# Early attention output turned by PE transposes and summed out of one bf16 bank, q and k turned by DMA and scored in one block from pair 8 on

## The chip, the cores and the metric

One core of a Trainium2 chip runs the whole program. The metric is device time in microseconds of one execution, given as the median of several runs. The engines named below are PE (matrix multiply; PEld is its weight load), DVE (vector), ACT (scalar), POOL (GpSimd) and SP (which only issues transfers here). They run side by side, each in the order of its own queue, and wait for one another on semaphores.

## The reference

Attention over 8 batches, 8 heads, 576 tokens and 64 dimensions, made of two parts, then a two-layer block without bias:

```
local:  softmax(q k^T / 8) v  over keys with |i - j| < 4
down:   q, k and v averaged over groups of 4 tokens; softmax(qd kd^T / 8) vd
x = local + repeat(down, 4)        # heads side by side: 4608 tokens x 512
h = x @ w_in                       # 512 -> 2048
out = (h - tanh(h)) @ w_out        # 2048 -> 512, f32
```

## The kernel before, in words

Work comes in 32 pairs of heads; pair p is batch p // 4, heads 2(p % 4) and the next. One pair (`attention(p)`) goes through these steps.

1. Load and cast. SP loads q and k (`qkn`) and v in overlapping windows (`vst`); `prep_v` casts v to bf16 (`vw`). `qkn` is cast to bf16 in `qr`: on any of three engines for pairs 0 to 3, on POOL at L515 after that.
2. Turn. q and k are needed with the dimension on the partitions. Pairs below `T_DMA` = 12 do that with nine PE transposes (L547) and two copies out of PSUM (L551). Later pairs do it with a DMA transpose (L531, `qT<-qr`) and one copy on ACT (L534).
3. Pool. Two adds (L564, L569, mostly POOL) make the averaged q and k, `qkd`.
4. Score. `s1` is eight matmuls of 120 query columns (L584) into two PSUM banks (token `t1`); `s2` is two more of 96 columns and four of 144 columns on `qkd` (L606) into two others (`t2`). Pairs from `NEW` = 12 on issue both as one block, `s12`.
5. Exp and mask. Pairs 0 to 3 add a bias to the scores on PE (L589). From pair 4 on, ACT takes the exponential out of PSUM into `E` (L622, L634, L637), and DVE then multiplies `E`, in SBUF, by a 0/1 `mask` (L626 with 960 columns, L641 with 192).
6. Output. 18 matmuls of 65 columns (L650, L657) give both outputs and the sums in two banks. DVE takes reciprocals (L670) and scales into `ln` (L672): five tiles of local output and two of the averaged one.
7. Turn back. Pairs below `X_DMA` = 12: nine matmuls (`back`, L683, L685, L692) multiply `ln` by an identity, and the averaged tiles by a matrix `up` that repeats each row four times, so that PSUM sums both in f32 in two banks; one copy (L720 on DVE or L721 on ACT) makes `xT`. Later pairs: a DMA transpose (L696, `lT<-ln`) and two adds (L703, L709) on DVE or POOL.

The dense block takes `xT` in nine blocks of 512 tokens: `mm1` (L734) 64 matmuls of 512 columns, then ACT's tanh (L742) and DVE's subtraction into `gT` (L745); `mm2` (L760) 64 matmuls, ACT's copy to `y` (L771) and a store (L774).

No order is written by hand. `Program` holds every step with an engine, an estimated duration and its dependencies. `order` plays the program with these estimates, with a latency for each engine (`LAT`), and with a cap on the PSUM banks that each kind of step may hold (`P.cap`: 6 of the 8 for pairs from 4 on, 4 for the dense block). `choice` lets it pick the engine. What comes out is a fixed queue for each engine. An engine whose next instruction isn't ready waits, even if later ones are.

Of the kernel before, what the change touches and what calls it, by code (L numbers as in the profile page):

```python
# [23 lines left out]
class Program:  # L24

    LAT = {"PE": 270, "ACT": 150, "DVE": 110, "POOL": 150, "SP": 50, "DMA": 2200}
    RING = 230

    def __init__(self):
        self.ops = []  # L30
        self.alternatives = {}
        self.slack = []
        self.soon = set()
        self.goal = set()
        self.ring = {}
        self.rings = {}
        self.touch = []
        self.use = []
        self.toks = []
        self.cap = {}  # L40
        self.last_write = {}
        self.readers = {}
# [66 lines left out]
    def order(self):  # L109
# [56 lines left out]
        for i in range(n):  # L166
            if left[i] == 0:
                make_ready(i)
        for step in range(n):
            best = None  # L170
            for eng, cand in ready.items():
                if not cand:
                    continue
                now = max(free.get(eng, 0.0), min(at[i] for i in cand))
                if eng == "PE":
# [8 lines left out]
                else:  # L184
                    pick = min((self.ops[i][4], i) for i in cand if at[i] <= now)[1]
# [12 lines left out]
            end = now + self.ops[i][1]  # L198
            want = [t for t in self.use[i] if t.first == i]
# [57 lines left out]
def kernel(  # L257
# [9 lines left out]
    nc = tc.nc  # L267
# [31 lines left out]
    mask = fixed("mask", [128, 576], BF16)  # L299
# [19 lines left out]
    up = lT[1].rearrange("p n c -> p (n c)")[:, 0:S]  # L319
    r = fixed("r", [128, 2, 7], FP32, 2)  # L320
    ln = fixed("ln", [128, 7, 128], BF16, 2)
# [31 lines left out]
    def c_up():  # L353

        GP.memset(up, 1.0)
        GP.affine_select(out=up, in_=up, compare_op=ALU.is_ge, fill=0.0,
                         base=0, pattern=[[1, S]], channel_multiplier=-4)
        GP.affine_select(out=up, in_=up, compare_op=ALU.is_ge, fill=0.0,
                         base=3, pattern=[[-1, S]], channel_multiplier=4)

# [8 lines left out]
    def c_mask():  # L369

        GP.memset(mask, 1.0)
        m4 = mask[:, 0:480].rearrange("p (t c) -> p t c", c=QW)
        for part, pat in ((m4, [[0, 4], [1, QW]]),
                          (mask[:, 480:576], [[1, 96]])):
            neg = [[-s, n] for s, n in pat]
            GP.affine_select(
                out=part, in_=part, compare_op=ALU.is_ge, fill=0.0,
                base=-1, pattern=neg, channel_multiplier=1)
            GP.affine_select(
                out=part, in_=part, compare_op=ALU.is_ge, fill=0.0,  # L380
                base=7, pattern=pat, channel_multiplier=-1)
        GP.affine_select(
            out=mask[:, 0:QW], in_=mask[:, 0:QW], compare_op=ALU.is_ge,
            fill=0.0, base=-4, pattern=[[0, QW]], channel_multiplier=1)
        GP.affine_select(
            out=mask[:, 480:576], in_=mask[:, 480:576], compare_op=ALU.is_ge,
            fill=0.0, base=99, pattern=[[0, 96]], channel_multiplier=-1)
# [80 lines left out]
    def pool_v4(p):  # L468
# [9 lines left out]
        op("POOL", 1150, a1, reads=[("v4", s)], writes=["v2"], pri=10 * p - 12)  # L478
        op("POOL", 750, a2, reads=["v2"], writes=[("vp", s)], pri=10 * p - 12)

    def pool_v(hb):
# [15 lines left out]
        op("ACT", 590, lambda: A.copy(  # L497
# [5 lines left out]
    def attention(p):  # L503
# [10 lines left out]
        if p >= NEARLY:  # L514
            op("POOL", 1300, lambda: GP.tensor_copy(  # L515
# [14 lines left out]
        if p >= T_DMA:  # L530
            P.dma("SP", 1740, lambda: nc.sync.dma_start_transpose(  # L531
                out=qT[s], in_=qr[s].rearrange("p a c -> p (a c)")), 1300, 72,
                  src=[("qr", s, 0), ("qr", s, 1)], dst=[("qT", s)], pri=-50, lead=500)
            op("ACT", 1250, lambda: A.copy(  # L534
# [3 lines left out]
        else:  # L538
            for a0, a1, tn, cn in ((0, 5, 290, 740), (5, 9, 230, 620)):
# [10 lines left out]
                def copy(fn, a0=a0, a1=a1, b16=b16):  # L550
# [5 lines left out]
                          ("DVE", cn, lambda copy=copy: copy(V.tensor_copy))][:1 + (p < NP)],  # L556
# [10 lines left out]
        def add2(eng):  # L567
            with nc.allow_low_precision("pooled q and k"):
                eng.tensor_tensor(out=qkd[s][:, 0:G],  # L569
                                  in0=half[:, :, 0, :],  # L570
                                  in1=half[:, :, 1, :], op=ALU.add)
        P.choice([(name, n1, lambda eng=eng: add1(eng)) for name, n1, _, eng in adders],
# [41 lines left out]
        if new:  # L614
            op("PE", 620, s12, slack=late, reads=qks + [("qkd", s)], fill=[t1, t2], pri=pri)
        else:
            op("PE", 420 * cold + 250 * (p < NP), s1, slack=late,
# [4 lines left out]
        op("ACT", 960, lambda: A.activation(  # L622
            out=e1, in_=two(t1)[:, :, 0:480], func=AF.Exp, scale=SCALE),
           drain=[t1], writes=[("E", e, 0)], pri=pri)
        if p >= NP:
            op("DVE", 950, lambda: V.tensor_tensor(  # L626
                out=e1, in0=e1,
                in1=mask[:, 0:480].unsqueeze(1).to_broadcast([128, 2, 480]),
                op=ALU.mult), reads=["mask"], writes=[("E", e, 0)], pri=pri)
        yield  # L630
        if not new:
            op("PE", 380 * cold + 100 * (p < NP), s2, slack=late, reads=qks + [("qkd", s)],
               fill=[t2], pri=pri)
        op("ACT", 310, lambda: A.activation(  # L634
            out=e2v, in_=two(t2)[:, :, 0:96], func=AF.Exp, scale=SCALE),
           drain=[t2], writes=[("E", e, 1)], pri=pri)
        op("ACT", 650, lambda: A.activation(  # L637
            out=e3, in_=two(t2)[:, :, 96:384], func=AF.Exp, scale=SCALE / 16.0),
           drain=[t2], writes=[("E", e, 2)], pri=pri)
        if p >= NP:  # L640
            op("DVE", 450, lambda: V.tensor_tensor(  # L641
                out=e2v, in0=e2v,
                in1=mask[:, 480:576].unsqueeze(1).to_broadcast([128, 2, 96]),
                op=ALU.mult), reads=["mask"], writes=[("E", e, 1)], pri=pri)
# [25 lines left out]
        op("DVE", 200, lambda: V.reciprocal(out=r[s], in_=blocks()[:, :, :, 64]),  # L670
           drain=[to], writes=[("r", s)], pri=pri)
        op("DVE", 1060, lambda: V.tensor_tensor(  # L672
# [6 lines left out]
        tb = P.psum(2, kind)  # L679

        def back():
            for half in range(2):
                T.matmul(two(tb)[:, half, 0:288], ln[s][:, 5, :], up[:, 288 * half:288 * half + 288],  # L683
                         start=True, stop=False)
            T.matmul(two(tb)[:, 1, 224:288], ln[s][0:16, 6, :], up[0:16, 0:64],  # L685
                     start=False, stop=False)
            for t in range(NT):
                q0, q1 = QW * t, QW * t + NQ[t]
                for half in range(2):
                    c0, c1 = max(q0, 288 * half), min(q1, 288 * half + 288)  # L690
                    if c0 < c1:
                        T.matmul(two(tb)[:, half, c0 - 288 * half:c1 - 288 * half],  # L692
                                 ln[s][0:NQ[t], t, :], ident[0:NQ[t], c0 - q0:c1 - q0],
                                 start=False, stop=(t == (2, NT - 1)[half]))
        if p >= X_DMA:
            P.dma("SP", 1350, lambda: nc.sync.dma_start_transpose(  # L696
# [4 lines left out]
            def join(eng):  # L701
# [12 lines left out]
            P.choice([("DVE", 1900, lambda: join(V)), ("POOL", 1400, lambda: join(GP))],  # L714
                     reads=[("lT", s)], writes=[("x", b, j)], pri=pri)
            return
        op("PE", 450 * cold, back, slack=late, reads=[("ln", s), ("lT", 1), "ident"],
           fill=[tb], pri=pri)
        xs = xT[j][:, b * S:(b + 1) * S].rearrange("p (n c) -> p n c", n=2)
        P.choice([("DVE", 720, lambda: V.tensor_copy(out=xs, in_=two(tb)[:, :, 0:288])),  # L720
                  ("ACT", 680, lambda: A.copy(out=xs, in_=two(tb)[:, :, 0:288]))],  # L721
                 drain=[tb], writes=[("x", b, j)], pri=pri)
# [4 lines left out]
    def mm1(kb, fc):  # L727
# [14 lines left out]
        op("ACT", 590, lambda: A.activation(  # L742
            out=u[us], in_=one(tok), func=AF.Tanh),
           drain=[tok], writes=[("u", us)], pri=DPRI)
        op("DVE", 670, lambda: V.tensor_tensor(  # L745
# [6 lines left out]
    def mm2(kb, i):  # L752
        ts, part, g = i // 4, i % 4, kb % 2
        if part == 0:
# [190 lines left out]
```

The softmax here doesn't subtract the row's maximum and nothing guards it: scores larger than these inputs give would overflow.

## Time and profile before

| What | Value |
|---|---|
| median of 7 runs | 333.99 us (332.46 to 339.42) |
| the profiled execution's own time | 336.19 us |
| its span in the trace | 334.2 us |
| PE busy | 315.2 us (94%) |
| DVE busy | 212.6 us (64%) |
| ACT busy | 202.9 us (61%) |
| POOL busy | 177.2 us (53%) |
| data moved | 59.80 MB, most of it before 225 us |
| first dense matmul | 25.52 us |
| last dense matmul ends | 329.81 us |

The span runs from the first instruction to the last. The first 25 us prepare batch 0. After that PE always has dense work behind it, with the attention of later batches between; from 250 us on it has dense work alone. Busy time of an engine includes time in which it is held inside an instruction, so a mean duration above the usual one is worth a look.

### The profile page before, as it was taken

To read this page: it belongs to the slowest core of one execution; us is meant where nothing else is said; L and a number is where in the kernel's file an instruction comes from. 1 tells how busy PE (TensorE), PEld (TensorE's weight loads), DVE (VectorE), ACT (ScalarE), POOL (GpSimd) and SP (SyncE) were. 2 spreads that over 40 slices of the span, in tenths; PEclk is the share of its full clock that TensorE was granted. 3 is DMA by queue.
4 is the path that set the end of the run, shared out by engine and by line. 5 is a ranking of instruction groups with operands and counts; after the bars stand their busy time and mean duration, and the time that the engine had idled before them with its cause. 6 is when DMAs were issued, how large, how long until landed. Compare 5 with 4: busy or idle time off the path is not lost.

```text
span 334.2 us, 6505 instructions
## 1 busy us (share of the span) xinstructions
PE 315.2 (94%) x2420; PEld 158.8 (48%) x2461; DVE 212.6 (64%) x330; ACT 202.9 (61%) x334; POOL 177.2 (53%) x211
## 2 busy tenths in 40 slices
PE   7989999999999999999696999999999999999994
PEld 2554555564444544444353445444444444444441
DVE  4868765479966969678969877758763344433300
ACT  3968864588777866687665466877544443444411
POOL 8564548859667698869887849887310000000000
PEclk9999999999999999999999999999999999999999
DMA  7999999989999999999999999982320001000021
GB/s 237 272 220 217 237 258 257 291 263 249 280 218 269 219 201 241 223 233 234 244 227 227 278 218 266 207 216 61 90 59 33 31 31 63 33 31 31 33 94 64
DMA packets 108862, 59.80 MB, mean 179 GB/s; under 512 B 86174, under 2 KB 96030, under 8 KB 108830
## 3 DMA queue, kind: packets, MB, share of 16 engines
q1 hardware_dynamic: 104318, 54.60, 69.8%
q0 software_dynamic: 4224, 4.19, 7.7%
q10 hardware_dynamic: 288, 0.59, 0.5%
q8 instruction: 19, 0.31, 0.4%
q14 instruction: 13, 0.11, 0.1%
HBM read 43.64 MB, written 9.44 MB: 159 GB/s over the span
## 4 chain that ended last, share of the span: by engine, by line
PE 72%; DVE 13%; DMA 6%; ACT 4%; POOL 2%; issue 2%; POOLq 0%; DVEq 0%; ACTq 0%
PE bank L734 31%; PE bank L760 29%; DMA lT<-ln 3%; DVE ln L672 3%; DVE E L626 3%; DMA w_out_sb<-in_moe_w_out_dram 3%; DVE E L641 3%; PE bank L650 3%; PE bank L584 2%; DVE gT L745 2%; PE bank L657 2%; ACT E L622 2%; DVE xT L703 1%; PE bank L692 1%; PE bank L683 1%
## 5 line engine op out<-in xcount | busy, mean ns | idle before, releaser
L734 PE MATMUL bank<-xT,w_in_sb 128*128 128x512 bf16 x557 | 143.7, 379 | 1.4 <-DVE gT L745 0.3
L760 PE MATMUL bank<-w_out_sb,gT 128*128 128x512 bf16 x555 | 141.6, 379 | 2.1 <-issue 0.6
L745 DVE TENSOR_TENSOR gT<-bank,u 128x512 bf16<-128x512 f32 x144 | 97.2, 685 | 64.1 <-ACT u L742 63.6
L742 ACT ACTIVATE u<-bank 128x512 f32<-128x512 f32 x144 | 85.9, 598 | 76.7 <-PE bank L734 73.8
L760 PEld LDWEIGHTS <-gT 128*128 128x128 bf16 x576 | 53.9, 98 | 62.8 <-issue 0.7
L734 PEld LDWEIGHTS <-w_in_sb 128*128 128x128 bf16 x576 | 53.9, 98 | 61.9 <-issue 0.5
L564 POOL TENSOR_TENSOR half<-qk 128x576 f32<-128x576 bf16 x28 | 32.1, 1145 | 21.0 <-ACT qk L551 12.3
L626 DVE TENSOR_TENSOR E<-E,mask 128x960 bf16<-128x960 bf16 x28 | 32.8, 1171 | 11.3 <-ACT E L622 11.1
L622 ACT ACTIVATE E<-bank 128x960 bf16<-128x960 f32 x32 | 31.1, 972 | 12.9 <-PE bank L584 12.8
L515 POOL CAST qr<-qkn 128x1152 bf16<-128x1152 f32 x28 | 32.2, 1151 | 9.9 <-DMA qT<-qr 6.7
L672 DVE TENSOR_TENSOR ln<-bank,r 128x896 bf16<-128x896 f32 x32 | 34.7, 1087 | 0.9
L771 ACT COPY y<-bank 128x512 f32<-128x512 f32 x36 | 21.1, 586 | 19.5 <-PE bank L760 19.0
L451 POOL CAST vw<-vst 128x640 bf16<-128x640 f32 x31 | 25.7, 833 | 8.5 <-DMA vst<-in_v_dram 8.5
L472 POOL TENSOR_TENSOR v<-v 72x512 f32<-72x512 f32 x20 | 25.4, 1270 | 2.8 <-DMA v<-in_v_dram 2.0
L534 ACT COPY qk<-qT 128x1152 bf16<-128x1152 bf16 x20 | 24.1, 1203 | 4.2 <-DMA qT<-qr 4.2
L650 PE MATMUL bank<-vw,E 128*128 128x65 bf16 x320 | 20.1, 194 | 4.8 <-DVE E L641 2.2
L569 POOL TENSOR_TENSOR qkd<-half 128x288 bf16<-128x288 f32 x29 | 21.8, 752 | 1.3 <-DVE r L670 0.4
L650 PEld LDWEIGHTS <-E 128*128 128x128 bf16 x320 | 16.6, 98 | 11.9 <-DVE E L641 2.9
L476 POOL TENSOR_TENSOR vp<-v 72x256 bf16<-72x256 f32 x20 | 14.5, 727 | 13.8 <-PE bank L657 13.6
L637 ACT ACTIVATE E<-bank 128x576 bf16<-128x576 f32 x32 | 21.1, 659 | 0.0
L703 POOL TENSOR_TENSOR xT<-lT 128x480 bf16<-128x480 bf16 x11 | 11.2, 1016 | 13.9 <-DMA lT<-ln 13.8
L641 DVE TENSOR_TENSOR E<-E,mask 128x192 bf16<-128x192 bf16 x28 | 18.0, 642 | 0.7 <-ACT E L634 0.7
(75 smaller groups left out, 220.8 us busy)
## 6 DMA issues: line engine op xcount, KB each, us to landing
vst<-in_v_dram SPq DMA_DIRECT2D x62, 160.0 KB, 5.2
qkn<-in_q_dram SPq DMA_DIRECT2D x32, 288.0 KB, 5.4
out_dram<-y SPq DMA_DIRECT2D x36, 256.0 KB, 4.6
qkn<-in_k_dram SPq DMA_DIRECT2D x30, 288.0 KB, 5.8
v<-in_v_dram SPq DMA_DIRECT2D x20, 288.0 KB
w_in_sb<-in_moe_w_in_dram POOLq DMA_DIRECT2D x4, 512.0 KB, 12.4
w_out_sb<-in_moe_w_out_dram POOLq DMA_DIRECT2D x4, 512.0 KB, 10.1
qkn<-in_k_dram ACTq DMA_DIRECT2D x2, 288.0 KB, 3.1
```

The lines of the kernel that those rows point to most:

```text
L451: P.choice([(eng, ns, lambda fn=fn: fn(out=vw[w][:, 2 * jj:2 * jj + 2, :, 0:64], in_=vst[s])) for eng, ns, fn in CAST_V[p >= NEARLY]], rea ...
L515: op("POOL", 1300, lambda: GP.tensor_copy(out=qr[s].rearrange("p a (h d) -> p h a d", h=2), in_=qkn[sn].rearrange("p h (a d) -> p h a d", ...
L564: eng.tensor_tensor(out=half, in0=four[:, :, 0:2, :], in1=four[:, :, 2:4, :], op=ALU.add)
L622: op("ACT", 960, lambda: A.activation(out=e1, in_=two(t1)[:, :, 0:480], func=AF.Exp, scale=SCALE), drain=[t1], writes=[("E", e, 0)], pri=pri)
L626: op("DVE", 950, lambda: V.tensor_tensor(out=e1, in0=e1, in1=mask[:, 0:480].unsqueeze(1).to_broadcast([128, 2, 480]), op=ALU.mult), reads= ...
L641: op("DVE", 450, lambda: V.tensor_tensor(out=e2v, in0=e2v, in1=mask[:, 480:576].unsqueeze(1).to_broadcast([128, 2, 96]), op=ALU.mult), rea ...
L650: T.matmul(two(to)[:, hh, 65 * t:65 * t + 65], E[e][:, c:c + 128], vw[w][:, 2 * jj + hh, t, :], start=True, stop=True)
L672: op("DVE", 1060, lambda: V.tensor_tensor(out=ln[s].rearrange("p n (h d) -> p h n d", d=D), in0=blocks()[:, :, :, 0:64], in1=r[s].unsqueez ...
L734: T.matmul(one(tok), w_in_sb[:, dc, fc * 128:(fc + 1) * 128], xT[dc][:, kb * 512:kb * 512 + 512], start=(dc == 0), stop=(dc == N_DC - 1))
L742: op("ACT", 590, lambda: A.activation(out=u[us], in_=one(tok), func=AF.Tanh), drain=[tok], writes=[("u", us)], pri=DPRI)
L745: op("DVE", 670, lambda: V.tensor_tensor(out=gT[g][:, fc, :], in0=one(tok), in1=u[us], op=ALU.subtract), drain=[tok], reads=[("u", us)], w ...
L760: T.matmul(one(tok), gT[g][:, fc, ts * 128:ts * 128 + 128], w_out_sb[:, fc, :], start=(fc == 0), stop=(fc == N_FF - 1))
```

## The change

- `back` for pairs 0 to 11 becomes seven PE transposes into one bank read as bf16 (five local tiles, then the averaged ones behind them). A small copy moves the averaged part to SBUF (`od`, DVE or ACT), and DVE adds it, each column repeated four times, to the local part: `xT`. `up` and its POOL instructions are gone.
- `T_DMA` goes from 12 to 8, and pairs 8 to 11 issue their scores as one block (`MERGE` = 8).
- The mask becomes a bias: from pair 4 on DVE adds 0 or -32768 to the scores in PSUM ahead of the exponential, no longer a product behind it. `mask` is gone.
- The additions of step 7's later form run on POOL only. `prep_v` may use ACT for every pair.
- The last 128 output rows are computed in two halves of 256 columns, each copied and stored by itself.
- The estimates of the planner are changed throughout. It now keeps POOL off while DVE runs one of the two pooling adds and the reverse (`port`), and the accumulators of `mm2` get a PSUM kind of their own with a cap of 3 ("y").

```diff
-    LAT = {"PE": 270, "ACT": 150, "DVE": 110, "POOL": 150, "SP": 50, "DMA": 2200}
+    LAT = {"PE": 235, "ACT": 145, "DVE": 110, "POOL": 140, "SP": 50, "DMA": 2000}
...
+                if eng == "DVE":
+                    now = max(free.get(eng, 0.0), min(
+                        max(at[i], port) if i in self.port else at[i] for i in cand))
+                elif eng == "POOL":
+                    now = max(now, port)
...
+        def band(tok, lo, hi):
+            part = two(tok)[:, :, 0:hi - lo]
+            V.tensor_tensor(out=part, in0=part, in1=bias[:, lo:hi].unsqueeze(1)
+                            .to_broadcast([128, 2, hi - lo]), op=ALU.add)
+        if p >= NP:
+            op("DVE", 1080, lambda: band(t1, 0, 480), reads=["bias"], fill=[t1], pri=pri)
...
-            op("DVE", 950, lambda: V.tensor_tensor(
-                out=e1, in0=e1,
-                in1=mask[:, 0:480].unsqueeze(1).to_broadcast([128, 2, 480]),
-                op=ALU.mult), reads=["mask"], writes=[("E", e, 0)], pri=pri)
...
+            op("DVE", 280, lambda: band(t2, 480, 576), reads=["bias"], fill=[t2], pri=pri)
...
-        tb = P.psum(2, kind)
+        tb = P.psum(1, kind)
+
+        def flat():
+            return one(tb).bitcast(BF16)[:, 0:S + G]
 
         def back():
...
+            for t in range(7):
+                q0, n = (QW * t, NQ[t]) if t < NT else (S + 128 * (t - NT), (128, 16)[t - NT])
+                T.transpose(flat()[:, q0:q0 + n], ln[s][0:n, t, :], ident[0:n, 0:n])
...
-            P.choice([("DVE", 1900, lambda: join(V)), ("POOL", 1400, lambda: join(GP))],
+            P.choice([("POOL", 1310, lambda: join(GP))],
...
+        P.choice([("DVE", 130, lambda: V.tensor_copy(out=od[s], in_=flat()[:, S:S + G])),
+                  ("ACT", 170, lambda: A.copy(out=od[s], in_=flat()[:, S:S + G]))],
+                 drain=[tb], writes=[("od", s)], pri=pri)
+        op("DVE", 610, lambda: V.tensor_tensor(
+            out=xT[j][:, b * S:(b + 1) * S].rearrange("p (g a) -> p g a", a=4),
+            in0=flat()[:, 0:S].rearrange("p (g a) -> p g a", a=4),
+            in1=od[s].unsqueeze(2).to_broadcast([128, G, 4]), op=ALU.add),
+           drain=[tb], reads=[("od", s)], writes=[("x", b, j)], pri=pri)
...
+        split = kb == NBLK - 1 and ts == 3
...
-    M2_FIRST, T_DMA, X_DMA, NEW, LATE = 16, 12, 12, 12, 0
+    M2_FIRST, T_DMA, X_DMA, NEW, LATE = 16, 8, 12, 12, 0
+    MERGE = 8
...
-    P.cap = {"b": 6, "d": 4}
+    P.cap = {"b": 6, "d": 4, "y": 3}
```

## The prediction, made before the changed kernel was run

> **What bounds the kernel now.** I began with busy time, took the span in stretches, then followed PE's waits back to their cause. The page's first table:
>
> ```profile
> PE 315.2 (94%) x2420; PEld 158.8 (48%) x2461; DVE 212.6 (64%) x330; ACT 202.9 (61%) x334; POOL 177.2 (53%) x211
> ```
>
> The busy table by stretch (columns: stretch, length, busy us of PE, PEld, DVE, ACT, POOL, then clock, DMA share, GB/s) shows where PE isn't full:
>
> ```profile
> 60.00:80.00 20.00, 18.75 (x208) 10.89 (x209) 13.09 (x21) 14.74 (x28) 15.00 (x17) 1.00 0.98 248
> ...
> 160.00:180.00 20.00, 16.04 (x152) 8.19 (x153) 17.06 (x25) 12.65 (x21) 16.14 (x18) 1.00 1.14 225
> 180.00:200.00 20.00, 18.20 (x124) 8.86 (x125) 17.35 (x23) 10.84 (x18) 13.86 (x16) 1.00 1.14 253
> ...
> 280.00:300.00 20.00, 19.95 (x92) 9.11 (x93) 7.83 (x12) 8.71 (x15) 0.00 (x0) 1.00 0.11 40
> ```
>
> From 250 us PE has dense work alone and is full, so time that PE loses or saves earlier moves the end one for one. From the first dense matmul (25.5) to the last (329.8) the rows leave PE about 10 us idle, 5.8 of it between 160 and 200, where DVE and POOL are busiest. PE's list of waits (us in total, times, longest):
>
> ```profile
> PE bank L650 <- DVE E L641: 2.2, 2, 1.5
> PE bank L650 <- DVE gT L745: 1.8, 1, 1.8
> PE bank L606 <- POOL qkd L569: 1.3, 1, 1.3
> ...
> PE bank L650 <- DVE E L626: 0.5, 1, 0.5
> ```
>
> The sum is 5.8 us. The queries on the single lines (min/median/max ns) and the timeline at 179 us say what is behind it:
>
> ```profile
> L626 DVE TENSOR_TENSOR E<-E,mask x28: 642/940/3479, 26.5 to 241.6; 128x960 bf16<-128x960 bf16 x28
> L641 DVE TENSOR_TENSOR E<-E,mask x28: 241/250/3804, 29.0 to 243.4; 128x192 bf16<-128x192 bf16 x28
> L745 DVE TENSOR_TENSOR gT<-bank,u x144: 627/691/693, 28.4 to 315.8; 128x512 bf16<-128x512 f32 x144
> L672 DVE TENSOR_TENSOR ln<-bank,r x32: 1029/1091/1093, 16.8 to 245.9; 128x896 bf16<-128x896 f32 x32
> ...
> 179.32 3.80 DVE L641 TENSOR_TENSOR E<-E,mask 128x192 bf16<-128x192 bf16 x1
> ...
> 183.18 0.20 PE L650 MATMUL bank<-vw,E 128*128 128x65 bf16 x1 [1.54 <-DVE E L641]
> ```
>
> A multiply of 192 columns needs 0.25 us and once took 3.80: in that time POOL ran five casts and adds without a gap. L626 and L641, whose two inputs lie in SBUF, vary fivefold and more; L745 and L672, with one input in PSUM, don't. By the page's means (1171 and 642 ns) the products hold DVE 28 x (1.171 - 0.642 + 0.642 - 0.250) = 26 us longer than at their least or usual time. The 1.8 us behind L745 is the same stall: at 158.71 an add L703, also with two SBUF inputs, took 2.96 us and L745 stood behind it.
>
> **What the Trainium skill says.** "SBUF — State Buffer", section "Who interferes with whom": a DVE instruction with two SBUF inputs takes its second through an interface shared with GpSimd and contends with GpSimd reads; with at most one SBUF input, outside the 2-port modes, it doesn't. The trace agrees (3.80 against 0.25 us; 693 ns at most for L745). "VectorE: DVE Perf Modes", section on the errata: an f32 tensor_tensor takes (N + 151)/0.96 ns. L745 and L672 give a slope of (1091 - 691)/384 = 1.04 ns and 158 ns fixed, the same. "TensorE: Matmul & The Clock Gate", Part 1: 55.8 ns between warm matmuls of 128 columns. The nine transposes from 68.07 to 68.57 us come to 55.6.
>
> **The change part by part.**
>
> *Mask to bias, 28 pairs.* DVE loses 28 x 1.171 + 28 x 0.642 = 50.8 us and gains two adds on PSUM. By the line above, 960 columns cost 158 + 1000 = 1.16 us and 192 cost 0.36, so 42.4 us. They have one SBUF input and can't be held by POOL. Without POOL's grip the products were cheaper (0.64 + 0.25): what goes is the stall, not work. On PE's path I count the 5.8 us above as gone; the bounds are 0 (the waits come back elsewhere) and the whole 10. What is late next: the exponential now waits for DVE, ACT's tanh instructions queue behind that exponential, and the score banks stay taken some 1.5 us longer. In trade, the outputs wait for ACT alone. I put 2 us of new PE waits, bounds 0 and 14 (second rival).
>
> *Turning back, 12 pairs.* On PE the old step takes 0.97 us at 76.77 and 0.96 at 82.35 up to the next dense matmul, 0.75 and 0.83 elsewhere; mean 0.88. Seven transposes take 6 x 0.056 = 0.33 plus one of 16 rows, whose neighbours showed gaps of 0.12 and 0.06, so 0.55 to 0.6. That is 0.3 a pair; 8 pairs lie behind 25.5 us: 2.4 us off PE. Bounds 1 and 4. DVE: 12 adds of 576 columns by the line 0.76 (9.1 us), against six copies L720 (4.5 us). ACT: six L721 (3.8) become nine copies of 144 columns, about 0.3 each by L634 (335 ns for 192). In steady state both lie beside dense work.
>
> *Turning by DMA in pairs 8 to 11.* Four times nine transposes leave PE: 4 x 0.50 = 2.0 us. ACT swaps nine copies L551 (5.8 us) for four L534 (4.8). SP and the DMA engines take four transposes more; at 147.13 and 156.98 it was 5 to 6 us from issue to the copy's start. In SP's new order the first stands behind pair 11's loads, issued in the old trace until 57.8 us. Then 5.5 + 1.2 (L534) + 1.14 (L564) + 0.67 (L569) + 0.4 for hand-overs puts pair 8's scores at 67 us. On PE they stand behind 156 dense matmuls and about 11 us of other work: 25.5 + 156 x 0.216 + 11 = 70.2. So it is covered by 3 us; if the queue is slower, PE stands.
>
> *One block of scores, pairs 8 to 11.* Two blocks cost 0.33 + 0.28 us and a gap of 0.1 each, 0.80; one block at 164.11 0.50 + 0.09, one at 174.04 0.8. I take 0.1 each, 0.4 us (0 to 0.8).
>
> *Other moves.* The nine adds L703/L709 on DVE (16.6 us) go to POOL (1.016 + 0.423 each, 13.0); 16 casts `vw` (0.833 each, 13.3) leave POOL for ACT (0.73 each, 11.7). DVE ends near 190 us, ACT near 211, POOL where it was. All lie beside dense work. `port` and the estimates issue nothing; they only order.
>
> *Start.* Off go `c_up` (1.9 us of POOL, hidden) and a bias instruction on DVE. Pair 3's last link becomes transposes, a copy and an add: +0.3 + 0.15 + 0.1 - 0.3, about +0.3 us (-1 to +1).
>
> *End.* The last copy has 256 columns (-0.2) and the last store half the bytes (-0.2); 32 matmuls of 256 cost about 0.05 more. -0.35 us.
>
> Sum: -2.4 - 2.0 - 0.4 - 5.8 + 2 + 0.3 - 0.35 = -8.65 us. The profiled execution took 336.19 us, 2 around its span of 334.2, and would take 327.5; it lies 2.2 above the median of 333.99, so against that median I say **325.3 us**.
>
> **The rivals.**
>
> *Stalls change place.* Pair 8 isn't ready at its place, or batch 2 comes late: the dense block may run only 256 matmuls ahead of it, and pair 11's transposes stand behind 242. For: DMA share is near or over 1 until 220 us, and SP's transposes took 1.3 to 3.8 us to issue. Against: in the whole trace PE waited 0.6 us for a DMA. A few such waits give back 4 to 6 us: 330 us.
>
> *Banks (slower than before).* A block of scores takes four banks and the pair before holds two for its outputs. Dense work gets two, for 1.16 + 0.36 us longer in each of 28 pairs, plus DVE's queue ahead of the bias. An `mm1` tile is filled in 0.86 us and needs some 1.5 to drain (598 + 685 ns and hand-overs). The gains without the 2 us of new waits are 10.65 us, so from 0.38 us of PE idle a pair nothing is left. At 0.5 a pair it is +14: 337.3 us. Against: PE waits only 0.3 us for L745's bank now, and `mm2` holds one bank for 3.5 us of work.
>
> *No effect.* The stalls were the planner's misjudgement and return with another order: 5 us of PE work less, 5 us more waiting: 334.
>
> **How the numbers follow.** Forecast 0.65 (own range 320 to 329), stalls change place 0.19, no effect 0.05, banks 0.11. The range, 318 to 334.5, reaches from all idle time gone (-10 in place of -3.8, start -1) to the no-effect case, and leaves out the banks case and a little of the low end. A measurement can tell about 0.5% (1.7 us) from no change; so faster 0.84, within 0.05, slower 0.11.
>
> **What would show it.** Right: the DVE adds at 1.16 and 0.36 us with hardly any spread; PE's waits on DVE's masks gone; PE idle between 160 and 200 under 2 us; dense matmuls still from about 25.8 us; an end about 8 us earlier. The turning back at 0.6 us a pair, pair 8's scores by 71 us without a wait. Wrong: PE waiting for ACT or DVE to give banks back at L731 or L764, for pair 8's `qT`, or for the averaged parts' copies; DVE adds as uneven as the products were; a start later by over 1 us.

## The result and the profile after

The changed kernel takes **338.27 us** (median of 12 runs, 335.77 to 344.19), the kernel before 334.17 in the same session (31 runs): ratio 1.0116, 95% interval 1.0086 to 1.0146. It is slower by 1.2%, where 325.3 us was forecast. Ratios here and below leave out disturbed executions, so they need not be the ratios of the medians. The profiled execution took 337.93 us, its span is 336.2. That of before lay 2 us above its median, so the two traces compared below lie only 1.74 us apart.

Table 1 of the page of the changed kernel, TensorE's row:

```profile
PE 313.8 (93%) x2374; PEld 159.2 (47%) x2414; DVE 193.5 (58%) x320; ACT 206.1 (61%) x348; POOL 171.1 (51%) x212
```

DVE lost 19 us, about as forecast (190). Of these, 8.4 come from the products that became adds (50.8 to 42.4 us); the nine adds L703/L709 that left DVE for POOL took 16.6 with them, and the new sums of step 7 brought some back. The groups of DVE's adds, and their smallest, median and largest time in ns with both sizes together, are as said: 1.16 and 0.36 us, and none of the 56 stretched.

```profile
L626 DVE TENSOR_TENSOR bank<-bank,bias 128x960 f32<-128x960 f32 x28 | 32.4, 1158 | 7.9 <-PE bank L586 7.9
L626 DVE TENSOR_TENSOR bank<-bank,bias 128x192 f32<-128x192 f32 x28 | 10.0, 357 | 2.5 <-PE bank L608 2.5
...
L626 DVE TENSOR_TENSOR bank<-bank,bias x56: 355/761/1167, 25.6 to 244.9; 128x960 f32<-128x960 f32 x28, 128x192 f32<-128x192 f32 x28
```

The end did not follow. Busy time by stretch (columns as in the prediction):

```profile
60.00:80.00 20.00, 19.89 (x124) 9.81 (x124) 9.91 (x16) 14.90 (x25) 10.95 (x12) 1.00 1.11 259
120.00:140.00 20.00, 17.33 (x153) 8.70 (x155) 9.42 (x15) 10.17 (x17) 16.76 (x20) 0.96 1.12 237
140.00:160.00 20.00, 18.27 (x107) 8.49 (x108) 12.67 (x22) 16.05 (x28) 14.95 (x17) 0.95 1.07 229
160.00:180.00 20.00, 18.26 (x172) 9.60 (x174) 11.50 (x19) 14.06 (x24) 17.06 (x20) 1.00 1.13 241
180.00:200.00 20.00, 17.40 (x144) 8.93 (x142) 13.77 (x22) 12.10 (x22) 13.23 (x17) 0.91 1.13 260
```

The hole of 160 to 200 us is only a little smaller (4.3 us without PE, 5.8 before), and a new one stands at 120 to 160, where the kernel before had PE busy for 38.9 of 40 us and this one for 35.6. DMA share is over 1 in all five. In three of these stretches the granted clock is under 1, which it never was there before. (Some 40 of the 1,152 dense matmuls have no record in either trace, so the holes of both look a little larger than they are.) PE's list of waits (us in total, times, longest) has other names, among them:

```profile
PE bank L731 <- DVE gT L742: 3.4, 2, 2.0
PE bank L608 <- POOL qkd L570: 2.1, 3, 1.1
PE bank L548 <- POOL qr L524: 2.0, 3, 0.8
PE bank L657 <- ACT E L642: 1.4, 3, 0.8
...
PE bank L650 <- ACT E L630: 0.9, 1, 0.9
PE bank L586 <- ACT E L630: 0.8, 1, 0.8
...
PE bank L650 <- ACT E L642: 0.4, 1, 0.4
```

Not one wait is for a mask. But L731 (`mm1`) now waits 3.4 us for a bank that DVE's L742 (`gT`, L745 before) empties. The timeline of the longest of these:

```profile
186.45 0.73 ACT L452 CAST vw<-vst 128x640 bf16<-128x640 f32 x1 [3.01 <-DMA vst<-in_v_dram]
...
187.08 0.59 ACT L739 ACTIVATE u<-bank 128x512 f32<-128x512 f32 x1
...
187.70 0.69 DVE L742 TENSOR_TENSOR gT<-bank,u 128x512 bf16<-128x512 f32 x1 [2.71 <-ACT u L739]
...
188.45 1.02 PE L731 MATMUL bank<-xT,w_in_sb 128*128 128x512 bf16 x4 [2.04 <-DVE gT L742]
```

ACT stood 3.01 us before a cast of v whose load had not landed; the tanh was behind it in ACT's queue, then came DVE's subtraction, which empties PE's bank, then PE. The page's chain of what ended last, which goes back from the last instruction to whatever released each step, says the same at large (shares of the span). First before:

```profile
PE 72%; DVE 13%; DMA 6%; ACT 4%; POOL 2%; issue 2%; POOLq 0%; DVEq 0%; ACTq 0%
```

and after:

```profile
PE 59%; DMA 20%; POOL 9%; issue 4%; ACT 3%; SPq 3%; DVE 2%; ACTq 0%; POOLq 0%; DVEq 0%
```

DVE left the chain (13% to 2%), and DMA with POOL behind it took its place (8% to 29%).

A small account of the two traces: the first dense matmul is at 25.52 us in both. The last ends at 329.81 before and 333.07 after, with 4.4 and 3.1 us behind it. So the tail gained some 1.3 us, and the stretch between grew by 3.2 although its work is some 4.8 us less (2.4 + 2.0 + 0.4 of the prediction): 8 us more are lost in it. Some 3.4 of these are matmuls at a low clock (an estimate, last section); the rest is waiting. The low clock isn't the main cause: in three other executions of the changed kernel the mean granted clock was 1.000, and they took 336.42, 336.78 and 338.62 us.

### The profile page after: what moved, and what is told of

The parts are those of the page before. It is cut to its first block, busy times and chain, and to the rows that moved or that the text cites. A ratio compares the mean times of both kernels' runs of the same rounds, so it can differ in the third digit from the quotient of the medians.

```text
span 336.2 us, 6452 instructions
## 1 busy us (share of the span) xinstructions
PE 313.8 (93%) x2374; PEld 159.2 (47%) x2414; DVE 193.5 (58%) x320; ACT 206.1 (61%) x348; POOL 171.1 (51%) x212
## 4 chain that ended last, share of the span: by engine, by line
PE 59%; DMA 20%; POOL 9%; issue 4%; ACT 3%; SPq 3%; DVE 2%; ACTq 0%; POOLq 0%; DVEq 0%
PE bank L764 28%; PE bank L731 23%; DMA vst<-in_v_dram 6%; DMA qkn<-in_k_dram 6%; DMA qT<-qr 4%; DMA w_out_sb<-in_moe_w_out_dram 2%; POOL half L565 2%; PE bank L586 2%; DMA lT<-ln 2%; PE bank L650 2%; POOL qr L516 2%; PE bank L657 1%; POOL qkd L570 1%; SPq L402 1%; DVE gT L742 1%
## 5 line engine op out<-in xcount | busy, mean ns | idle before, releaser
L731 PE MATMUL bank<-xT,w_in_sb 128*128 128x512 bf16 x554 | 140.1, 382 | 5.6 <-DVE gT L742 3.4
L742 DVE TENSOR_TENSOR gT<-bank,u 128x512 bf16<-128x512 f32 x144 | 96.5, 688 | 83.5 <-ACT u L739 83.2
L764 PE MATMUL bank<-w_out_sb,gT 128*128 128x512 bf16 (+1 forms) x575 | 138.6, 376 | 2.9 <-issue 1.0
L764 PEld LDWEIGHTS <-gT 128*128 128x128 bf16 x592 | 56.3, 98 | 64.3 <-issue 3.3
L731 PEld LDWEIGHTS <-w_in_sb 128*128 128x128 bf16 x576 | 54.2, 98 | 68.1 <-issue 6.5
L626 DVE TENSOR_TENSOR bank<-bank,bias 128x960 f32<-128x960 f32 (+1 forms) x56 | 41.7, 758 | 10.5 <-PE bank L586 7.9
L535 ACT COPY qk<-qT 128x1152 bf16<-128x1152 bf16 x24 | 29.1, 1219 | 12.2 <-DMA qT<-qr 7.8
L776 ACT COPY y<-bank 128x512 f32<-128x512 f32 (+1 forms) x37 | 21.3, 575 | 21.4 <-PE bank L764 21.4
L696 POOL TENSOR_TENSOR xT<-lT 128x480 bf16<-128x480 bf16 x20 | 20.2, 1010 | 20.1 <-DMA lT<-ln 18.8
L452 ACT CAST vw<-vst 128x640 bf16<-128x640 f32 x17 | 12.5, 734 | 17.3 <-DMA vst<-in_v_dram 17.3
L650 PE MATMUL bank<-vw,E 128*128 128x65 bf16 x320 | 20.0, 196 | 1.3 <-ACT E L630 0.9
L570 POOL TENSOR_TENSOR qkd<-half 128x288 bf16<-128x288 f32 x30 | 19.9, 664 | 1.9 <-PE bank L495 1.0
L670 DVE RECIPROCAL r<-bank 128x14 f32<-128x14 f32 x32 | 7.7, 240 | 22.5 <-PE bank L657 22.0
L650 PEld LDWEIGHTS <-E 128*128 128x128 bf16 x320 | 16.3, 99 | 7.8 <-ACT E L630 1.5
```

Of the source, the lines that this page charges most:

```text
L535: op("ACT", 1095, lambda: A.copy(out=full.rearrange("p (g a) i -> p g a i", a=A9), in_=qT[s].rearrange("p a (g i) -> p g a i", i=2)), read ...
L626: V.tensor_tensor(out=part, in0=part, in1=bias[:, lo:hi].unsqueeze(1) .to_broadcast([128, 2, hi - lo]), op=ALU.add)
L650: T.matmul(two(to)[:, hh, 65 * t:65 * t + 65], E[e][:, c:c + 128], vw[w][:, 2 * jj + hh, t, :], start=True, stop=True)
L731: T.matmul(one(tok), w_in_sb[:, dc, fc * 128:(fc + 1) * 128], xT[dc][:, kb * 512:kb * 512 + 512], start=(dc == 0), stop=(dc == N_DC - 1))
L742: op("DVE", 610, lambda: V.tensor_tensor(out=gT[g][:, fc, :], in0=one(tok), in1=u[us], op=ALU.subtract), drain=[tok], reads=[("u", us)], w ...
L764: T.matmul(one(tok)[:, 0:n], gT[g][:, fc, ts * 128:ts * 128 + 128], w_out_sb[:, fc, cols:cols + n], start=(fc == 0), stop=(fc == N_FF - 1))
```

## The experiments

The first suspicion was that one queue. It led to a question about orders in general.

### Is it the casts that moved to ACT?

Edit, with every queue kept in its order (the engine that issues 16 casts is swapped, its place in the planner's books is not); the second kernel lets the planner order anew with the casts on POOL alone:

```
-              [("POOL", 770, GP.tensor_copy), ("ACT", 620, A.copy)]]
+              [("POOL", 770, GP.tensor_copy), ("ACT", 620, GP.tensor_copy)]]   # same order
+              [("POOL", 770, GP.tensor_copy)]]                                 # new order
```

> The changed kernel with every queue in its order, except that the 16 v casts which ACT runs in it are issued at the same places of the plan on POOL. Queue theory (ACT stands 17.3 us at casts whose v has not landed, with tanh and exponentials behind them): ACT's waits for v go to zero, PE's 4.0 us of waits for gT and 2.7 us for E shrink to under 1.5 us together, no stretch with a clock under 0.97 remains, and the time falls by 5 to 8 us from 338.3, to 330 to 333. Transfer theory (v and the turned q and k land late because of four more DMA transposes; the casts only show it): another instruction waits in their place, under 2 us are gained, 336.5 to 339. Estimate theory (the plan is too tight in all places): 336 to 339. Bias theory (the add ahead of the exponential holds banks and ACT): no change, 337.5 to 339.

Measured 1.0135 (1.0085 to 1.0185) against before: no gain over 1.0116. ACT's waits for v are gone, but the mean granted clock of the profiled execution was 0.98 against 0.99, and PE's list of this run begins:

```profile
PE bank L731 <- ACT y L776: 4.0, 2, 3.8
PE bank L548 <- POOL qr L524: 3.2, 2, 2.1
PE bank L764 <- DMA w_out_sb<-in_moe_w_out_dram: 2.9, 1, 2.9
```

Another late transfer took over: ACT now stood up to 4.7 us before `qT` (L535), with copy `y` behind it.

> The changed kernel with POOL as the only choice for the v casts from pair 4 on, and the plan made anew. Queue theory: 329 to 333, as in the run with the same plan, give or take another order. Transfer, estimate and bias theory: 336 to 339.

Measured 1.0095 (1.0059 to 1.0131); ACT waits 20.6 us for `qT` instead. The queue theory falls: the place of the stall moves, the time stays. (The second run has a new order besides.)

### Is it q and k by DMA in pairs 8 to 11?

```
-    M2_FIRST, T_DMA, X_DMA, NEW, LATE = 16, 8, 12, 12, 0
+    M2_FIRST, T_DMA, X_DMA, NEW, LATE = 16, 12, 12, 12, 0
```

> The changed kernel with q and k turned by DMA from pair 12 on, as before; all else as changed, the plan made anew. Transfer theory: four transposes less (3.4 us of 16 engines) bring v and qT forward, ACT's waits for v fall from 17 to under 9 us, and the time goes to 330 to 334. Queue theory: PE has 2 us of transposes more, ACT still runs v casts and waits for v; 337 to 340, less only as far as ACT's waits for v fall with the new order. Estimate and bias theory: 338 to 341.

Measured 1.0085 (1.0048 to 1.0123). On the 334.17 us of before that is 337.0: the 330 to 334 of the transfer theory did not come. But the interval overlaps that of the change, and this is a new order too, so it settles little more.

### Is it the estimates?

The diff also changes four DMA estimates: the latency and the times for q and k and for v are shortened, that for the weights is lengthened. They issue nothing; the planner only places things by them. Three kernels try them: the old ones put back in the changed kernel; the same with that of v raised; and the new ones in the kernel before, with nothing else:

```
# changed kernel, old estimates        # changed, raised        # before, new estimates
LAT "DMA": 2000 -> 2200                2200                     2200 -> 2000
T_QK, T_V, T_W = 760, 850, 3000
     -> 800, 1000, 2850                800, 1150, 2850          -> 760, 850, 3000
```

> The changed kernel planned with the DMA estimates of the kernel before (latency 2200, q and k 800, v 1000, weights 2850). No instruction is added or removed, only the order and the choice of engines are new. Estimate theory: casts and turned operands are placed later, ACT's waits for v fall under 6 us and the time goes to 329 to 333. Queue theory: it gains exactly as far as ACT's waits for v fall; with 17 us still there, 337 to 339. Transfer and bias theory: 336 to 339.

Measured 0.9924 (0.9882 to 0.9966): 1.9% off the changed kernel without touching its work, and faster than both.

> The changed kernel planned with DMA estimates as before (latency 2200, q and k 800, weights 2850), but 1150 for a v load in place of 850 (1000 before). Measured, q loads of pairs 12 to 31 follow each other every 7.5 us; the changed estimates add up to about 6.9 us a pair, the old ones to 7.3, these to 7.6. Pace theory (instructions that need transfers are queued too early because the plan takes the transfers for faster than they are): at least as good as with the old DMA estimates, 329 to 332.5. If only some other property of the old estimates' order helped, 333 to 338.

Measured 1.0137 (1.0081 to 1.0193), 338.8 us and over both ranges: longer estimates are not better as such.

> The kernel before, with nothing but the four DMA estimates of the change (latency 2000, q and k 760, v 850, weights 3000). Pace theory: its own work unchanged, but consumers of transfers queued earlier, so PE waits more: 337 to 342, slower by 1 to 2%. Structure theory (the estimates hurt only together with the new bias, turns or casts): 333 to 336.

Measured 1.0316 (1.0272 to 1.0361). The new numbers alone, in the kernel before, cost 10.6 us, more than either theory allowed.

### Parts of the change, ordered anew

The mask turned to a bias in the kernel before, and that with the PE transposes of `back` as well, old estimates in both:

```
-            op("DVE", 950, lambda: V.tensor_tensor(out=e1, in0=e1, in1=mask ..., op=ALU.mult) ...
+            op("DVE", 1080, lambda: band(t1, 0, 480), reads=["bias"], fill=[t1], pri=pri)
...
+                T.transpose(flat()[:, q0:q0 + n], ln[s][0:n, t, :], ident[0:n, 0:n])   # second kernel only
```

> The kernel before with the mask as a bias added in PSUM ahead of the exponential, estimates as before (1080 and 280 for the two adds). My prediction's step (5.8 us of PE waits on DVE's products gone, 2 us of new ones): 329 to 332. Bank and queue theory (score banks held 1.5 us longer, ACT waits for DVE ahead of its tanh): 335 to 341. Planner theory (stalls change place with any new order): 332 to 337 with PE's waits near the 13.6 us of before, named otherwise.

Measured 1.0016 (0.9982 to 1.0049): no change. This is the kinder reading: the median of all its runs is 337.05 us against 334.61, 0.7% more. The waits for masks are gone, and `mm1` (L731 in this kernel) waits 3.7 us for `gT` banks, 0.3 before.

> As the run before it, and the output of pairs 0 to 11 turned back by seven PE transposes and summed by DVE out of one bf16 bank. My prediction's steps: 2.4 us of PE work less in the dense part, +0.3 at the start, so 1.5 to 2.5 us faster than with the bias alone. If saved PE work is eaten by waits: within 1 us of it.

Measured 1.0089 (1.0058 to 1.0120): with more work taken from PE, it is no faster. By the interval it is slower than the run above; by the medians of all runs (337.18 us) the two are alike. These waits for `gT` are 5.5 us.

### The prices at an unchanged order

In these two every queue keeps the order of the kernel before; work is only left out, the greater part of each mask in the first, the averaged part of the early outputs in the second.

```
-                out=e1, in0=e1,
-                in1=mask[:, 0:480].unsqueeze(1).to_broadcast([128, 2, 480]),
+                out=e1[:, :, 0:8], in0=e1[:, :, 0:8],
+                in1=mask[:, 0:8].unsqueeze(1).to_broadcast([128, 2, 8]),
...                                                 # L641 likewise
```

> The kernel before, every queue in its own order, with each of the 56 mask products of VectorE cut to 8 columns per head (0.3 to 0.4 us in all instead of up to 3.80; it leaves out most of the mask). The order is the same, the products are nearly gone. If the prediction's price holds at an unchanged order, TensorE's waits for L641 and L626 (2.7 us) go, those for L745 behind the products shrink, and the end comes 3 to 6 us earlier (328.5 to 331.5 us, ratio 0.982 to 0.991). If another resource sets the pace of the middle of the kernel whatever VectorE does (DMA, ScalarE), the time stays within 1 us (ratio 0.997 to 1.003).

Measured 0.9954 (0.9924 to 0.9985): 1.5 us (0.5 to 2.5); the medians of all runs differ by 1.0. DVE's busy time fell from 212.6 to 190.6, and PE's waits for masks are gone. Of the 5.8 us that the prediction counted, this kernel could take 4.0; the 1.8 behind the add L703, which it keeps, stay. Why not 4.0? PE's list of this run now begins with two entries, of which the first was 1.3 before:

```profile
PE bank L606 <- POOL qkd L569: 2.1, 1, 2.1
PE bank L650 <- DVE gT L745: 1.8, 1, 1.8
```

Its timelines of POOL and of PE at that wait:

```profile
176.49 1.26 POOL L472 TENSOR_TENSOR v<-v 72x512 f32<-72x512 f32 x1 [2.58 <-DMA v<-in_v_dram]
177.71 0.67 POOL L569 TENSOR_TENSOR qkd<-half 128x288 bf16<-128x288 f32 x1
...
178.44 0.30 PE L606 MATMUL bank<-qkd 64*128 64x144 bf16 x4 [2.08 <-POOL qkd L569]
```

and the same place in the kernel before:

```profile
177.01 1.27 POOL L472 TENSOR_TENSOR v<-v 72x512 f32<-72x512 f32 x1 [2.00 <-DMA v<-in_v_dram]
178.24 1.08 POOL L569 TENSOR_TENSOR qkd<-half 128x288 bf16<-128x288 f32 x1
...
179.38 0.30 PE L606 MATMUL bank<-qkd 64*128 64x144 bf16 x4 [1.27 <-POOL qkd L569]
```

PE would have been there 1.75 us earlier (178.44 - 2.08 = 176.36 against 179.38 - 1.27 = 178.11) and got through 0.94 earlier: 0.8 us went into a longer wait, because the load of v ahead of `qkd` in POOL's queue came only 0.5 us earlier. The chain's first row agrees: DVE down from 13 to 2%, DMA up from 6 to 17%, in the same order of instructions. (Each trace is one execution: this one took 334.30 us, 1.2 over the median of its kernel, that of before 336.19.)

```profile
PE 61%; DMA 17%; POOL 10%; issue 4%; ACT 3%; DVE 2%; SPq 1%; POOLq 0%; ACTq 0%; DVEq 0%
```

The second kernel leaves work out of PE itself:

```
-            for half in range(2):
-                T.matmul(two(tb)[:, half, 0:288], ln[s][:, 5, :], up[:, 288 * half:288 * half + 288],
-                         start=True, stop=False)
-            T.matmul(two(tb)[:, 1, 224:288], ln[s][0:16, 6, :], up[0:16, 0:64], start=False, stop=False)
...
-                                 start=False, stop=(t == (2, NT - 1)[half]))   # the six matmuls that stay
+                                 start=True, stop=True)
```

> The kernel before, every queue in its own order, without the three matmuls L683 and L685 of each early output (12 pairs, 36 matmuls; it leaves out the averaged part of the early outputs). At 288 and 64 columns these issue in some 0.30 us a pair, 3.6 us in all. If time that TensorE saves early moves the end one for one at an unchanged order, the time falls by 3 to 4 us (ratio 0.988 to 0.991). If saved work is given back at the next wait (TensorE runs ahead into data that aren't there yet), it falls by less than 1 us.

Measured 0.9923 (0.9895 to 0.9951): 2.6 us (1.6 to 3.5). The medians of all runs, 333.11 us against 334.01, differ by 0.9 only, so this size is loose. And the three matmuls take more than the 0.30 us a pair that was expected. The timeline of the kernel before:

```profile
76.77 0.42 PE L683 MATMUL bank<-lT,ln 128*128 128x288 bf16 x2
...
77.25 0.43 PE L692 MATMUL bank<-ident,ln 120*128 120x120 bf16 x6
77.74 1.24 PE L734 MATMUL bank<-xT,w_in_sb 128*128 128x512 bf16 x5
```

and the same place of this run:

```profile
75.96 0.43 PE L692 MATMUL bank<-ident,ln 120*128 120x120 bf16 x6
76.45 1.24 PE L734 MATMUL bank<-xT,w_in_sb 128*128 128x512 bf16 x5
```

The step went from 0.97 to 0.49 us, and from the start of L683 to that of L692 it is 0.47 or 0.48 us in all 12 pairs: 5.7 us in all, of which about half or less arrived. The two traces show where the rest went. When PE began the scores of a pair at 44.21 us, it was 2.4 us ahead of the kernel before (46.65). Then it waited for the averaged q and k:

```profile
44.06 0.73 POOL L451 CAST vw<-vst 128x640 bf16<-128x640 f32 x1 [6.51 <-DMA vst<-in_v_dram]
...
46.98 0.30 PE L606 MATMUL bank<-qkd 64*128 64x144 bf16 x4 [2.33 <-POOL qkd L569]
```

In the kernel before, the same cast, which stands ahead of `qkd` in POOL's queue, began at 44.08 and these matmuls at 46.92, without a wait:

```profile
44.08 0.73 POOL L451 CAST vw<-vst 128x640 bf16<-128x640 f32 x1 [6.32 <-DMA vst<-in_v_dram]
...
46.92 0.30 PE L606 MATMUL bank<-qkd 64*128 64x144 bf16 x4
```

The load of v came no earlier, so the whole lead was spent in waiting for it, and from 48 to 52 us PE's granted clock was 0.57. At 61 us the two kernels are level (a block of `mm2` at 60.94 against 60.79, where the kernel before had waited 0.6 us for weights). The five early outputs behind that arrive in full: 5 x 0.48 = 2.4 us, and the last of them is 2.5 us ahead (87.23 against 89.72).

### How much does an order weigh?

One estimate of the planner is nudged by 1%. The work stays; what changes is the order and, with it, the engine that `choice` picks for a few steps.

```
-    T_QK, T_V, T_W, W_PRI, NEARLY = 800, 1000, 2850, 32, NP
+    T_QK, T_V, T_W, W_PRI, NEARLY = 800, 990, 2850, 32, NP
```

> The kernel before with one estimate of the planner nudged, T_V 1000 to 990 (1%): the same instructions, but from pair 2 on nearly every queue in another order. If the time of such a kernel depends on the accident of the order, the time differs from before by 1% or more in either direction (3 us or more). If the order between equally good plans does not matter, the time is within 0.5%.

Measured 1.0190 (1.0144 to 1.0236). A number changed by 1% costs 6.3 us. Its page and PE's first wait:

```profile
PE 317.1 (94%) x2420; PEld 159.7 (47%) x2461; DVE 221.8 (66%) x337; ACT 202.2 (60%) x333; POOL 176.8 (53%) x205
```

```profile
PE bank L734 <- DVE gT L745: 5.1, 3, 3.4
```

> The changed kernel with one estimate of the planner nudged, T_V 850 to 860 (1%): the same instructions in another order. If the 338.3 us of the changed kernel are the accident of one order, this one differs from it by 1% or more (under 335 or over 341.5 us). If they are the price of the changed work or of shorter estimates as such, it stays at 337 to 340 us.

Measured 1.0177 (1.0128 to 1.0227), 0.6% over the changed kernel. The median of 339.95 us lies where the changed work or the new estimates as such were to put it, not where an accident of one order was.

> The kernel before with T_V nudged from 1000 to 1010 (1%): the same instructions in another order. If the kernel before is simply one of the better orders of its structure, this one is slower by 1 to 3%, as the nudge to 990 was (ratio 1.01 to 1.03). If the nudge to 990 was one bad case, this one lies within 0.5% of before.

Measured 1.0209 (1.0167 to 1.0251): the nudge to 990 was not one bad case.

> The changed kernel with the old DMA estimates, T_V nudged from 1000 to 990. If the gain of 0.8% with the old estimates belongs to the structure (less work on TensorE, no mask products on the path), it stays: ratio 0.985 to 0.998. If it belongs to that one order, the ratio goes to 1.005 to 1.02.

Measured 0.9932 (0.9907 to 0.9957), median 331.38 us: the gain stays.

> The changed kernel with the old DMA estimates, T_V nudged from 1000 to 1010. The same two theories as for the nudge to 990: structure 0.985 to 0.998, accident of the order 1.005 to 1.02; the mean of the three orders of this structure against the mean of the three orders of the kernel before tells what the change of the work is worth, 1 to 2% if the prediction's sums of saved work are right.

Measured 1.0058 (1.0021 to 1.0095): just inside the range of the accident, with an interval that reaches below it. So the gain of single orders isn't safe. The measure set here beforehand, the mean of three orders against the mean of three, is 0.9971 / 1.0133 = 0.984: 1.6%, within the 1 to 2% said.

> The changed kernel with the old DMA estimates, every queue in its own order, the v casts that stand on ScalarE issued on GpSimd. ScalarE's waits for v (12.1 us in 5 instances, longest 5.3) go. If these cost the end anything at this order, the time falls by 1 to 3 us below the 332.3 us of the same order with the casts on ScalarE. If they lie beside other work, it stays within 1 us, and if GpSimd's casts hold back the averages of q and k behind them, it rises by 1 to 4 us.

Measured 0.9987 (0.9959 to 1.0015), 0.6% over the same order with the casts on ACT, about 2 us: in this order POOL is the worse place for them, though ACT waited 12.1 us before them. (The intervals of the two just touch.)

Two more supply partners, so that both structures have run at six equal sets of DMA estimates (only `T_V`, `T_QK`, `T_W` and the DMA latency, as above).

> The kernel before with T_V raised from 1000 to 1150, the partner of the changed kernel at the same four DMA estimates (1.0137 against before). If the changed work is worth 1 to 2.5% at equal estimates, this one is at 1.023 to 1.04. If the changed structure is no faster and the four pairs so far fell by chance, it is as likely under 1.0137 as over it.

Measured 1.0159 (1.0113 to 1.0205), under the expected range. It is over its partner (1.0137), but by less than the noise.

> The kernel before with the four DMA estimates of the change and T_V 860, the partner of the changed kernel at the same estimates (1.0177 against before). If the changed work is worth 1 to 2.5% at equal estimates, this one is at 1.027 to 1.043; otherwise it is as likely under 1.0177 as over it.

Measured 1.0271 (1.0236 to 1.0307), just within the range for a gain by the work.

All pairs, each time against the kernel before:

| DMA estimates | structure before | structure changed | changed / before |
|---|---|---|---|
| old | 1 | 0.9924 | 0.992 |
| old, `T_V` 990 | 1.0190 | 0.9932 | 0.975 |
| old, `T_V` 1010 | 1.0209 | 1.0058 | 0.985 |
| old, `T_V` 1150 | 1.0159 | 1.0137 | 0.998 |
| new | 1.0316 | 1.0116 | 0.981 |
| new, `T_V` 860 | 1.0271 | 1.0177 | 0.991 |

At equal DMA estimates the changed structure is the faster in six of six, clear of noise in five. The mean of the last column is 0.987, with a standard deviation of 0.8 points, so -1.3% with a 95% interval of 0.9 either way (taking the six as independent draws): 4.4 us. In each column the two rows with new estimates lie 1.3 to 1.5% over the mean of the four with old ones (1.0294 against 1.0140; 1.0147 against 1.0013). And the kernel before is the best of four orders of its own structure at old estimates, 1.4% under their mean. The measured 1.2% is then 1.4 (a favourable order lost) - 1.3 (the work) + 1.3 (the new estimates) - 0.3 (the order drawn is a bit better than the mean of its two) = 1.1. This is bookkeeping with the means of the table, which closes by construction. With a scatter of about 1 point in each column, four orders give a mean to some 1.5 points (an estimate, 95%), so the share of each term is rough. Surer is that the same work at slightly other estimates gave 1 to 1.0316 before and 0.9924 to 1.0177 after.

What stays open: why the new estimates cost. With two orders a column against four, that they do so as such, and not by the orders drawn, is only likely. The other new numbers of the diff (latencies of PE, ACT and POOL, durations, `port`, the cap on `y`) were never separated from the changed work; they are in the -1.3%.

## Why the prediction was wrong, step by step

**Right, and seen in the profile.** The adds at 1.16 and 0.36 us, free of POOL's grip, as "SBUF — State Buffer" of the Trainium skill, section "Who interferes with whom", says of an instruction with one SBUF input: at most 1.17 us in 56, where the products went to 3.8. DVE at 193.5 us (190 said). First dense matmul as early as before. Turning back in 0.52 us a pair up to the next dense matmul (41.70 to 42.23, 81.21 to 81.74), against 0.88. Pair 8's scores at 72.4 us without a wait, its averaged q and k done at 67.5 (67 said, place at 70.2). The tail better, by 1.3 us where 0.35 was said.

**"That is 0.3 a pair; 8 pairs lie behind 25.5 us: 2.4 us off PE."** Right as work, as just said. But "time that PE loses or saves earlier moves the end one for one" holds only in part: leaving out the 36 `up` matmuls, 5.7 us of PE, moved the end by 2.6 (1.6 to 3.5) at an unchanged order, so by some 0.45 for one (0.3 to 0.6), and by less if the medians are taken. The traces split it: what seven pairs had saved by 61 us was gone there, spent on the wait for a load of v and at a low clock, and what the other five saved arrived one for one. The 2.0 and 0.4 us of pairs 8 to 11 rest on the same rule and were not tried by themselves.

**"On PE's path I count the 5.8 us above as gone."** Mis-sized. (The 5.8 of the list is not quite the 5.8 without PE between 160 and 200 us: the 0.5 for L626 lies before 130.) At an unchanged order the part of it that could be tried, 4.0 us, was worth 1.5 (0.5 to 2.5). A wait in PE's list was read as time to be had, but another deadline can stand close behind it. DMA share stood at 1.14 in that very stretch, and at the place shown the load of v ahead of `qkd` took 0.8 of a lead of 1.75 us. The 1.8 us behind L745, whose cause is the add L703 on DVE, was not tried by itself.

**"I put 2 us of new PE waits, bounds 0 and 14 (second rival)."** The named new waits came, and larger: L650, L657 and L586 for exponentials 3.5 us, L731 for `gT` banks 3.4 (0.3 before). The second is the place that the *banks* rival named, and its 337.3 us is within 1 us of the measured time. That is luck, for its mechanism isn't there: the wait came twice and not in each of 28 pairs, and the longest began with a late load ahead of ACT's tanh.

**"Sixteen casts ... lie beside dense work."** Looked wrong, and wasn't what counted: the same order with the casts on POOL was no faster in the changed kernel, and slower by 0.6% with the old estimates.

**"`port` and the estimates issue nothing; they only order."** This is the step that failed. The order was priced at zero, while a nudge of 1% in one estimate costs the kernel before 6.3 us, and the four new DMA estimates 10.6. Every item of the sum changed the order too, and was costed as if it did not. Of the forecast -8.65 us the work gave about -4.4 (1.3%, 0.4 to 2.2); the order took back about 8 by the bookkeeping above: some 4.7 for leaving a favourable order (1.4%) and 4.5 with the new estimates (1.3%), less 1.0.

The rival *no effect*, "the stalls were the planner's misjudgement and return with another order", had the mechanism, with a chance of 0.05, but stopped at zero, as if another order could return no more than the waits that the change took away. The trace of before did not show the spread; it couldn't, since it shows one order.

## What to carry to other kernels

Where a planner turns estimates into fixed queues, a change is two changes, of the work and of the order. Before crediting either, nudge an estimate by 1% a few times on both versions: here single orders of one kernel differ by up to 2.1% at nearly the same estimates, more than the change of the work was worth (1.3%). And price a wait by the next deadline behind it, not by its length: with DMA share over 1, a stall taken from DVE was in good part handed to a load (1.5 of 4.0 us arrived).

## What the runs showed of the hardware

The granted clock fell in places of the changed kernel where TensorE was only thinly busy. Stretches of 2 us (columns: stretch, length, busy us and count of PE, clock, DMA share, GB/s), where lines are left out between the two places:

```profile
134.00:136.00 2.00, 1.12 (x9) 1.00 1.05 261
136.00:138.00 2.00, 1.18 (x29) 1.00 1.03 311
138.00:140.00 2.00, 1.84 (x7) 0.61 1.16 208
140.00:142.00 2.00, 2.00 (x6) 0.53 0.94 308
142.00:144.00 2.00, 2.00 (x11) 1.00 1.19 268
...
186.00:188.00 2.00, 0.41 (x2) 1.00 1.09 320
188.00:190.00 2.00, 1.23 (x5) 0.91 1.13 350
190.00:192.00 2.00, 2.00 (x14) 0.50 1.14 248
192.00:194.00 2.00, 1.95 (x29) 0.73 1.05 266
```

After 4 us in which PE was busy for 2.3 (134 to 138) or 1.6 (186 to 190), it ran the next 2 to 4 us at about half clock, fully busy. Four matmuls of 512 columns took 1.86 us, one every 0.43, where four at 188.45 (shown above) took 1.02, one every 0.22:

```profile
189.80 1.86 PE L764 MATMUL bank<-w_out_sb,gT 128*128 128x512 bf16 x4 [0.32 <-DVE gT L742]
```

By the clock column I estimate that these dips cost (0.39 + 0.47) x 2 and (0.09 + 0.50 + 0.27) x 2 us, 3.4 in all, on top of the waits themselves. "TensorE: Matmul & The Clock Gate" of the Trainium skill, Part 1, gives 426.7 ns for such a matmul at the low clock, which agrees; it speaks of an idle window of some 3.4 us, while the longest single wait here was 2.04. In the kernel without the `up` matmuls the one wait of 2.33 us was followed by the same: PE busy for 1.67 of the 4 us from 44, then 4 us at a clock of 0.57.

How thin is too thin, these runs don't show. In the kernel with the cut masks PE was busy for only 1.92 of the 4 us from 176, with a wait of 2.08 in them, and in the kernel before for 2.19 of the 4 from 160, and the clock stayed at 1.00. So a stall can cost more than its length, which the prediction had not reckoned with, but it need not.
